# GpSimd waits for VectorE's ramps, and VectorE no longer asks whether GpSimd is idle: a change in the planner of a two-layer attention and gMLP kernel

## The chip, the core and the metric

The kernel runs on one core of a Trainium2 chip. The metric is the device time of one execution in microseconds (us). Five engines are named as the profile names them: PE (TensorE, with PEld for its weight loads), DVE (VectorE), ACT (ScalarE), POOL (GpSimd) and SP (SyncE, which issues the DMAs here). Each engine takes its instructions strictly in the order in which they stand in its stream; an instruction may wait for semaphores that other engines raise.

## What is computed

Two layers, each of multi-query attention (32 heads of 16, one shared key and value head) and a gMLP block, on a sequence of 2048 rows of 512:

```python
def _A_ref(x, wq, wk, wv, wo):
    q = (x @ wq).reshape(B, S, H, Dh).transpose(0, 2, 1, 3)
    k = x @ wk
    v = x @ wv
    scores = jnp.einsum('bhqd,bkd->bhqk', q, k) * Dh ** (-0.5)
    p = _softmax(scores, axis=-1)
    o = jnp.einsum('bhqk,bkd->bhqd', p, v)
    return o.transpose(0, 2, 1, 3).reshape(B, S, H * Dh) @ wo

def _B_ref(x, w_in, w_sp, b_sp, w_out):
    z = _gelu(jnp.einsum('bsd,df->bsf', x, w_in))
    z1 = z[..., :Fh].copy()
    z2 = _layernorm(z[..., Fh:], axis=-1)
    g = jnp.einsum('ts,bsf->btf', w_sp, z2) + b_sp[None, :, None]
    return jnp.einsum('bsf,fd->bsd', z1 * g, w_out)

x = x + _A_ref(_layernorm(x), A_wq, A_wk, A_wv, A_wo)
x = x + _B_ref(_layernorm(x), B_w_in, B_w_sp, B_b_sp, B_w_out)
...
```

The last two lines run twice. With 32 heads, 2048 queries and 2048 keys a layer has 2048 blocks of 128 keys by 512 scores: 4096 in all, each of which needs its exponential.

## The kernel before

**Two ways to an exponential.** TensorE makes a block of scores in a PSUM bank (line 1252, `issue_pack`). Most blocks go to ScalarE, which reads one bank or two neighbouring ones and writes exponentials into slots of the buffer `Pb` (line 1460, `do_exp`). The others go to VectorE and GpSimd. VectorE first reads the bank, adds a constant and writes int16 whose bits are those of a bf16 close to the exponential (line 1374, `first_fn`, called "A" below; it sets the PSUM bank free). Two shifted copies of that slot are then made from SBUF to SBUF (line 1379, `ramp_fn`): these are the **ramps**, tag "S" in the planner. Either VectorE or GpSimd can make a ramp, one slot at a time (128x512) or, where two sources and two free slots lie side by side, two at a time (128x1024, a **pair**; `commit_ramp`, `ramp_pair`). Three weighted copies stand for one exponential, so a block on this way costs TensorE three products with the values and not one (line 1515, `do_pv`).

**The planner.** Nothing is ordered by hand. At build time the class `Sched` plays the whole kernel through with a cost for each operation, and the class `Kernel` decides at each moment what an idle engine takes next (`run` calls `step_act`, `step_dve`, `step_pool`, `step_pe` and `step_sp`). What it commits becomes the stream of that engine; the waits are derived from each task's dependencies (`deps`, and `extra` for reused buffers). In the plan each engine has a time from which it is free (`s.free`). On the chip only the order and the waits are left of it.

**The shared port.** The planner takes VectorE's ramps, its LayerNorm outputs `xn` and `z2n` (the tuple `PORT`) to need something that GpSimd's work needs too. When VectorE commits such a task, GpSimd is planned as occupied until its end (lines after `port =` in `commit`), and VectorE takes a ramp only at a moment when GpSimd is idle in the plan (`s.free["pool"] <= s.t`, line 1711 and its twin further down in `step_dve`). Two thresholds on GpSimd's planned backlog go with that: over `POOL_TOP` VectorE takes a pair ahead of all other work; over `POOL_MAX` it takes any ramp, but only if it has nothing else to do. In the streams, however, no wait keeps GpSimd from starting while VectorE makes its ramps.

**What surrounds it.** GpSimd's stream also holds the reciprocal roots (lines 605 and 606), `xn` (line 628), `z2n` (line 1016) and the last gate products (line 1150). SyncE transposes `xn` by DMA (line 529) for the MLP (lines 988 and 1034), whose gelu runs on ScalarE. The spatial product of the gMLP (line 1095) is added up by VectorE (line 1103). The next layer's attention begins while the last pass of the MLP runs. Where TensorE would be too idle the planner puts in products with a zero operand (line 1634, `keep_warm`). `ACT_LOW` says at which planned backlog of ScalarE TensorE may issue fewer than four blocks of scores at once, `PV_FREE` how many slots of `Pb` must be free before a new accumulation bank is opened, and `SHARE` which part of the blocks goes the VectorE way while TensorE has much else to do.

Of the kernel before, what the change touches and what calls it, by code (L numbers as in the profile page):

```python
# [65 lines left out]
class Task:  # L66
# [3 lines left out]
    def __init__(self, eng, cost, fn, deps=(), prio=5, gate=None, hook=None, mode="full", alts=None, tag=""):  # L70
        self.eng = eng
        self.cost = cost
        self.fn = fn
        self.deps = [d for d in deps if d is not None]
        self.succ = []
        self.prio = prio
        self.ready = 0.0
        self.start = None
        self.done = None
        self.key = None  # L80
        self.val = 0
        self.gate = gate
        self.hook = hook
        self.mode = mode
        self.extra = []
        self.alts = alts
        self.sem = None
        self.armed = False
        self.tag = tag
        self.ramp = None  # L90


class Sched:
# [3 lines left out]
    def __init__(self, nc):  # L97
        self.nc = nc
        self.prog = {e: [] for e in ENGS}
        self.free = {e: 0.0 for e in ENGS}  # L100
        self.cnt = {e: 0 for e in ENGS}
        self.know = {e: {} for e in ENGS}
        self.snap = {}
        self.arm = {e: [] for e in ENGS}
        self.events = []
        self.seq = 0
        self.pe_mode = None
        self.dma_last = [None] * self.NDMA
        self.dma_n = [0] * self.NDMA
        self.t = 0.0  # L110
        self.left = 0
        self.log = []
        self.pe_log = []
        self.after = []
        self.busy = {e: 0.0 for e in ENGS}

    def event(self, t):
# [45 lines left out]
    def commit(self, task, eng=None):  # L163
        t = self.t
        eng = eng or task.eng
        task.eng = eng
        if task.alts is not None:
            task.cost, task.fn = task.alts[eng]
        task.start = t
        if task.hook is not None:  # L170
            task.hook(task)
        cost = task.cost() if callable(task.cost) else task.cost
        occ, lat = cost
        if eng == "pe" and task.mode != self.pe_mode:
            occ += 110
            self.pe_mode = task.mode
        port = eng == "dve" and task.tag in PORT
        if port:
            occ += max(0.0, self.free["pool"] - t)
        end = t + occ  # L180
        self.free[eng] = end
        if port:
            self.free["pool"] = max(self.free["pool"], end)
        self.busy[eng] += occ
        task.done = end + lat
        waits = self._waits(eng, task)
        if eng == "sp":
            k = min(range(self.NDMA), key=lambda i: (self.dma_last[i].done if self.dma_last[i] else -1.0))
            prev = self.dma_last[k]
            if prev is not None:  # L190
                waits += self._wait_on(eng, prev)
            self.dma_n[k] += 16
            task.key, task.val = ("dma", k), self.dma_n[k]
            self.dma_last[k] = task
        else:
            self.cnt[eng] += 1
            task.key, task.val = eng, self.cnt[eng]
        s = dict(self.know[eng])
        if s.get(task.key, 0) < task.val:
            s[task.key] = task.val  # L200
        self.snap[(task.key, task.val)] = s
        self.prog[eng].append((waits, task.fn, task.key, task))
        self.log.append((eng, t, end, task.tag))
        if eng == "pe":
            self.pe_log.append((t, end))
        self.left -= 1
        for s_ in task.succ:
            s_.nopen -= 1
            if s_.nopen == 0:
                self._arm(s_)  # L210
        self.event(end)
        self.event(task.done)
        while self.after:
            self.after.pop(0)()
        return task
# [164 lines left out]
class Kernel:  # L380
# [1 line left out]
    SCORE_CAP = 6  # L382
    WSP_FROM = 25000
    NPS = 32
    PV_FREE = 8
    KT_ACT = 16
    CREDIT = 2
    A_TWO = 0
    KEEP = 8
    PAIRS = 0  # L390
    POOL_TOP = 4000
    HOLD = 200
    A_ADJ = 1
    CAP_LINE = 8000
    RAMP_SHARE = 0.32
# [4 lines left out]
    GP_PRIO = 0.95  # L400
    SP_PRIO = 3.5
    NROT = (2, 2)
    SHARE = 0.32
    SHARE_HI = 0.34
    PE_LINE = 5000
    WARM = 0.6
# [4 lines left out]
    ACT_LOW_R = 0  # L411
    PV_R = 0
    RAMP_SHARE1 = 0.0
    ACT_LOW = 1400
    POOL_MAX = 1400
    DVE_MAX = 1500
    DVE_HIGH = 1800
# [757 lines left out]
    def pack_ready(self):  # L1175
# [4 lines left out]
        room = min(4, len(av), self.score_cap() - self.score_held)  # L1180
        low = self.ACT_LOW if A.full or A.layer == 0 else self.ACT_LOW_R
        if room < (self.FILL_MIN if A.full or A.layer == 0 else self.FILL_R) or room < 4 and self.act_backlog() > low:
# [30 lines left out]
    def issue_pack(self, A, blks, deps, bs):  # L1213
        s = self.s
        k = len(blks)

        x = (self.RAMP_SHARE, self.RAMP_SHARE1)[A.layer] if not A.full else self.SHARE if self.pe_line() > self.PE_LINE else self.SHARE_HI
        self.credit = min(self.credit + k * x, self.CREDIT) if x else 0.0
# [12 lines left out]
        for act in itertools.combinations(sorted(bs, key=lambda b: b.i), len(aj)):  # L1231
            runs = sum(1 for x, y in zip(act, act[1:]) if y.i != x.i + 1)
            rest = sorted([b.i for b in bs if b not in act][:nd] + pend)
            key = (runs - self.A_ADJ * sum(1 for x, y in zip(rest, rest[1:]) if y == x + 1), sum(b.i for b in act))
            if best is None or key < best[0]:
# [242 lines left out]
    def pv_candidate(self):  # L1478
# [5 lines left out]
        for u in self.pv_order:  # L1484
# [4 lines left out]
            if r:  # L1489
                if u.bank is None and (not self.banks.avail() or held >= self.attns[min(self.ai, 1)].nrot_now() and freep >= self.PV_FREE):  # L1490
                    continue
# [101 lines left out]
    def pack_due(self):  # L1593
# [19 lines left out]
        e4 = known[3] if len(known) > 3 else t + 1e5  # L1613
        dry = max(t, s.free["act"]) + 450.0 * len(self.act_q) - self.ACT_LOW
        w = min(e4, max(e2, dry))
# [92 lines left out]
    def step_dve(self):  # L1708
        s = self.s
        k = None  # L1710
        if s.free["pool"] <= s.t + self.PORT_WAIT and self.backlog("pool") > self.POOL_TOP:

            k = self.ramp_pair("dve")
        if k is None:
            k = s.pick("dve", lambda k: k.alts is None or "pool" not in k.alts)

        if k is None and s.free["pool"] <= s.t + self.PORT_WAIT and self.backlog("pool") > self.POOL_MAX:
            k = s.pick("dve")
        if k is None:
            return False  # L1720
        if k.ramp is not None:
            self.commit_ramp(k, "dve")
        else:
            s.commit(k, "dve")
        return True
# [15 lines left out]
    def step_pool(self):  # L1741
        s = self.s
        k = None
        if s.t < s.free["dve"] <= s.t + self.HOLD and self.backlog("pool") > self.POOL_TOP:
            return False
# [138 lines left out]
```

## Time and profile before

| | |
|---|---|
| median of three runs | 1646.38 us (1645.14 to 1647.46) |
| the profiled execution | 1641.84 us, of which the span is 1640.1 us |
| granted TensorE clock | 0.987 |
| busy: PE, DVE, ACT, POOL | 1480.0, 1452.0, 1441.8, 1139.3 us |
| blocks on ScalarE | 923 instructions of two, 956 of one |
| blocks on VectorE's way | 1294, hence 2588 ramps |
| ramps on VectorE | 371 pairs, 111 single |
| ramps on GpSimd | 576 pairs, 583 single |
| zero products (line 1634) | 204 |

"Busy" is the time in which at least one instruction of an engine is recorded as running. VectorE's records overlap: the next one starts some 0.08 us before the one ahead ends, so a row's mean duration is longer than what the instruction adds to the stream. A releaser behind an arrow is what ended an engine's idle time.

### The profile page before, as it was taken

The page shows a single profiled execution, that of the slowest core. Times are in us where ns is not written, and L with a number is a line of the kernel's source. Part 1 is how long each engine was busy: PE and PEld are TensorE (multiplying, and loading weights), DVE is VectorE, ACT ScalarE, POOL GpSimd, SP SyncE. Part 2 cuts the span into 40 slices and gives each one's busy share as a digit, 9 for nine tenths or more (in the row PEclk, how much of TensorE's full clock was granted, in tenths as well). Part 3 has the DMA queues.
Part 4 walks back from the last instruction along what each step waited for, and adds up shares of the span by engine and source line. Part 5 has one row for each costly group of instructions (what it writes and reads, how often), then busy time and mean ns, then how long its engine had stood idle before and what let it go on. Part 6 is the DMA issues. An engine that isn't in the chain of part 4 may idle for free.

```text
span 1640.1 us, 36572 instructions
## 1 busy us (share of the span) xinstructions
PE 1480.0 (90%) x13974; PEld 498.6 (30%) x14104; DVE 1452.0 (89%) x2624; ACT 1441.8 (88%) x2052; POOL 1139.3 (69%) x1410
## 2 busy tenths in 40 slices
PE   6999799999999899989988988999889998999998
PEld 3233232222322223223543322322223222322334
DVE  7899979999799897987874999899997999899977
ACT  5999989999899898987479999899998999899950
POOL 5777768777587677875113767687786877677747
PEclk9999999999999899999999999999999999999999
DMA  9000000100010010101120000020100011101111
GB/s 215 10 8 5 5 10 17 31 20 18 11 27 14 14 27 14 27 14 30 30 44 10 5 5 8 8 46 18 14 15 14 17 24 21 20 14 27 17 33 62
DMA packets 123994, 39.74 MB, mean 24 GB/s; under 512 B 116272, under 2 KB 123312, under 8 KB 123824
## 3 DMA queue, kind: packets, MB, share of 16 engines
q1 hardware_dynamic: 123824, 37.41, 11.3%
q8 instruction: 115, 1.88, 0.5%
q14 instruction: 55, 0.45, 0.1%
HBM read 6.98 MB, written 2.10 MB: 6 GB/s over the span
## 4 chain that ended last, share of the span: by engine, by line
PE 38%; DVE 31%; ACT 22%; issue 4%; POOL 3%; DMA 1%; POOLq 0%; SPq 0%; DVEq 0%; ACTq 0%
ACT Pb L1460 21%; DVE Pb L1374 16%; PE ps_all L1252 11%; PE ps_all L1515 11%; DVE Pb L1379 8%; PE ps_all L1095 6%; PE ps_all L988 3%; PE ps_all L1034 3%; DVE gp L1103 2%; POOL z L1150 2%; PE ps_all L1160 1%; DVE ln_st L614 1%; PE ps_all L773 1%; DVE oT L830 1%; DMA z<-xn 1%
## 5 line engine op out<-in xcount | busy, mean ns | idle before, releaser
L1460 ACT ACTIVATE Pb<-ps_all 128x512 bf16<-128x512 f32 (+1 forms) x1879 | 1345.6, 856 | 78.9 <-PE ps_all L1252 61.8
L1379 POOL TENSOR_SCALAR Pb<-Pb 128x512 int16<-128x512 int16 (+1 forms) x1159 | 987.3, 852 | 340.0 <-DVE Pb L1374 178.1
L1374 DVE TENSOR_SCALAR Pb<-ps_all 128x512 int16<-128x512 f32 x1294 | 842.6, 680 | 86.7 <-PE ps_all L1252 78.5
L1252 PE MATMUL ps_all<-Q,kT 32*128 32x512 bf16 x4096 | 583.6, 388 | 92.8 <-ACT Pb L1460 35.5
L1515 PE MATMUL ps_all<-Pb,V 128*32 128x512 bf16 x6684 | 526.6, 390 | 15.4 <-DVE Pb L1379 4.4
L1252 PEld LDWEIGHTS ps_all<-Q,kT 32*128 32x128 bf16 x4096 | 153.2, 91 | 620.0 <-ACT Pb L1460 361.4
L1379 DVE TENSOR_SCALAR Pb<-Pb 128x1024 int16<-128x1024 int16 (+1 forms) x482 | 260.1, 562 | 9.2 <-PE ps_all L1515 7.9
L1095 PE MATMUL ps_all<-wstr,z 128*128 128x512 bf16 x748 | 194.9, 380 | 19.1 <-issue 5.9
L1515 PEld LDWEIGHTS ps_all<-Pb,V 128*32 128x32 bf16 x6684 | 119.0, 95 | 235.2 <-issue 114.2
L1103 DVE TENSOR_TENSOR gp<-ps_all,gp 128x512 f16<-128x512 f32 x168 | 112.6, 684 | 15.5 <-PE ps_all L1095 14.8
L1095 PEld LDWEIGHTS ps_all<-wstr,z 128*128 128x128 bf16 x840 | 67.1, 97 | 106.6 <-DVE Pb L1374 16.4
L605 POOL TENSOR_SCALAR ln_rs<-ln_mv 128x1 f32<-128x1 f32 (+2 forms) x48 | 10.8, 230 | 86.3 <-DVE ln_mv L615 85.5
L830 DVE CAST oT<-ps_all 128x512 bf16<-128x512 f32 x64 | 43.4, 680 | 19.4 <-PE ps_all L1515 19.4
L1160 PE MATMUL ps_all<-w_out,z 128*128 128x512 bf16 x212 | 55.2, 380 | 3.4 <-POOL z L1150 0.9
L988 PE MATMUL ps_all<-w_in,xnT 128*128 128x448 bf16 x256 | 53.2, 363 | 1.9 <-DVE Pb L1374 1.1
L1048 ACT ACTIVATE z<-ps_all 128x512 bf16<-128x512 f32 (+1 forms) x60 | 31.3, 566 | 22.3 <-PE ps_all L1034 22.3
L1034 PE MATMUL ps_all<-xnT,w_in 128*128 128x512 bf16 (+2 forms) x274 | 50.2, 336 | 0.3
L1001 DVE BATCH_NORM_STATS2 st<-z 128x6 f32<-128x448 bf16 x64 | 36.8, 604 | 11.7 <-ACT z L993 11.5
L614 DVE BATCH_NORM_STATS2 ln_st<-X 128x6 f32<-128x512 bf16 x64 | 43.1, 680 | 3.7 <-DMA X<-in_A_x_dram 3.5
L1103 DVE TENSOR_TENSOR gp<-ps_all,bspc 128x512 f16<-128x512 f32 x56 | 38.3, 686 | 7.0 <-PE ps_all L1095 6.5
L605 POOL TENSOR_SCALAR rs<-mv 128x4 f32<-128x4 f32 (+2 forms) x10 | 2.3, 232 | 58.5 <-DVE mv L1003 58.5
L773 PE MATMUL ps_all<-z,wq 128*128 128x128 bf16 x512 | 40.9, 224 | 1.6 <-DVE Pb L1374 1.3
(69 smaller groups left out, 711.1 us busy)
## 6 DMA issues: line engine op xcount, KB each, us to landing
out_dram<-X SPq DMA_DIRECT2D x16, 128.0 KB, 1.7
w_in<-in_B_w_in_dram SPq DMA_DIRECT2D x1, 1792.0 KB, 13.0
X<-in_A_x_dram SPq DMA_DIRECT2D x3, 512.0 KB, 7.5
bspc<-in_B_b_sp_dram SPq DMA_DIRECT2D x8, 128.0 KB, 3.3
w_out<-in_B_w_out_dram SPq DMA_DIRECT2D x1, 896.0 KB, 12.5
wstr<-in_B_w_sp_dram SPq DMA_TRANSPOSE x40, 4.0
X<-in_A_x_dram SPq DMA_DIRECT2D x2, 256.0 KB, 3.2
wq<-in_A_wq_dram SPq DMA_DIRECT2D x1, 512.0 KB, 4.5
```

The costliest lines, as they stand in the source:

```text
L614: a = self.dve(c_ps(512), lambda e, t=t: e.bn_stats(st[:, t, :], X[:, t, :]), [dep], prio, tag="lnst")
L830: ev = Task("dve", c_ps(512), lambda e, u=u, k=k: e.tensor_copy(self.oT[:, k, :], self.ps32[:, u.bank.i, :]), [self.oT_use[k]], 0.2, tag=" ...
L988: ins = e.matmul(self.ps32[:, b, 0:448], self.xnT2[:, buf, kd, o:o + P], self.w_in[:, kd, FH + h * 448:FH + (h + 1) * 448], start=(kd == 0 ...
L1034: ins = e.matmul(self.ps32[:, b, i * nq:(i + 1) * nq], self.w_in[:, kd, f * P:(f + 1) * P], self.xnT2[:, buf, kd, 0:nq], start=(kd == 0), ...
L1095: ins = e.matmul(self.ps32[:, b, :], self.z2[:, (s0 + i) % 8, f * P:(f + 1) * P], self.wstr[:, sl[i // 4][1] + i % 4, :], start=(i == 0), ...
L1103: return Task("dve", c_ps(512), lambda e: e.tensor_tensor(self.gp[:, tc, f, :], self.ps32[:, bank(), :], src, ALU.add), dps, 1.05, tag="gp")
L1160: ins = e.matmul(self.ps32[:, b, :], self.z1[:, tc, f, o:o + P], self.w_out[:, f, :], start=(f == 0), stop=(f == NF - 1))
L1252: ins = e.matmul(self.ps32[:, jb[i].i, :], self.kT[32 * j:32 * j + 32, u.half, kt * P:(kt + 1) * P], q, tile_position=(32 * j, 0), start=T ...
L1374: return lambda e: e.tensor_scalar(self.Pi[:, dst():dst() + k, :], self.ps32[:, bank:bank + k, :], EBIAS + lo, lo, op0=ALU.add, op1=ALU.max)
L1379: return lambda e: e.tensor_scalar(self.Pi[:, dst():dst() + k, :], self.Pi[:, src():src() + k, :], lo, 1.0, op0=ALU.add, op1=ALU.mult)
L1460: return e.activation(self.Pb[:, s0:s0 + n, :], self.ps32[:, b0:b0 + n, :], ACTF.Exp, scale=ESCALE)
L1515: ins = e.matmul(self.ps32[32 * j:32 * j + 32, u.bank.i, :], self.V[:, var, kt, :], self.Pb[:, sl.i, :], tile_position=(0, 32 * j), start= ...
```

## The change

Only the planner and its constants are edited; no instruction gets a new form.

1. `commit`: when VectorE commits a port task, GpSimd is planned as occupied until that task's result is ready (`end + lat` in place of `end`), and the task is remembered as `port_task`. The next task that GpSimd commits gets it as a dependency, which becomes a semaphore wait in GpSimd's stream. If VectorE commits several ramps before GpSimd's next task, only the last is waited for, which covers the ones ahead of it.
2. `step_dve` asks for `s.pool_end` in place of `s.free["pool"]`, so that the hold that VectorE itself put on GpSimd doesn't end its turn. `pool_end` is set to the end of GpSimd's task when one is committed. The last of the added lines, which is not under an `if`, sets it to 0.0 again at the end of that step of every commit, for any engine. Whenever `step_dve` runs, `pool_end` is therefore 0.0, and both conditions on it hold always. In the same way nothing is ever added to a ramp's planned cost for GpSimd's remaining work.
3. Constants: `POOL_TOP` from 4000 to 3000, with a new `POOL_ON` of 3000 that is used while a `port_task` is open; `PV_FREE` from 8 to 6; `SHARE` from 0.32 to 0.33; `ACT_LOW` from 1400 to 1200.

```diff
         if port:
-            occ += max(0.0, self.free["pool"] - t)
+            occ += max(0.0, self.pool_end - t)
         end = t + occ
         self.free[eng] = end
         if port:
-            self.free["pool"] = max(self.free["pool"], end)
+            self.free["pool"] = max(self.free["pool"], end + lat)
+            self.port_task = task
+        if eng == "pool":
+            self.pool_end = end
+        if eng == "pool" and self.port_task is not None:
+
+            task.extra.append(self.port_task)
+            self.port_task = None
+        self.pool_end = 0.0
...
-    PV_FREE = 8
+    PV_FREE = 6
...
-    POOL_TOP = 4000
+    POOL_TOP = 3000
     HOLD = 200
+    POOL_ON = 3000
...
-    SHARE = 0.32
+    SHARE = 0.33
...
-    ACT_LOW = 1400
+    ACT_LOW = 1200
...
     def step_dve(self):
         s = self.s
         k = None
-        if s.free["pool"] <= s.t + self.PORT_WAIT and self.backlog("pool") > self.POOL_TOP:
+
+        if s.pool_end <= s.t + self.PORT_WAIT and self.backlog("pool") > (self.POOL_TOP if s.port_task is None else self.POOL_ON):
 
             k = self.ramp_pair("dve")
         if k is None:
             k = s.pick("dve", lambda k: k.alts is None or "pool" not in k.alts)
 
-        if k is None and s.free["pool"] <= s.t + self.PORT_WAIT and self.backlog("pool") > self.POOL_MAX:
+        if k is None and s.pool_end <= s.t + self.PORT_WAIT and self.backlog("pool") > self.POOL_MAX:
             k = s.pick("dve")
```

What it makes of the streams can be counted in the two built programs, without a time:

| | before | after |
|---|---|---|
| VectorE: pairs, single ramps | 371, 111 | 204, 645 |
| VectorE: unbroken runs of ramps (of one, of two, longer) | 344 (230, 100, 14) | 571 (308, 249, 14) |
| VectorE: A | 1294 | 1304 |
| GpSimd: pairs, single ramps | 576, 583 | 234, 1087 |
| GpSimd: instructions that wait for VectorE | 867 | 1220 |
| ScalarE: exponentials of two blocks, of one | 923, 956 | 885, 1022 |
| TensorE: products with the values | 6684 | 6704 |
| TensorE: products with zero | 204 | 132 |

More of the change, by code (lines that the diff above doesn't have):

```diff
@@ L182, in commit @@
         if port:
-            self.free["pool"] = max(self.free["pool"], end)
+            self.free["pool"] = max(self.free["pool"], end + lat)
[4 more added lines that the diff above has]
+            task.extra.append(self.port_task)
+            self.port_task = None
+        self.pool_end = 0.0
         self.busy[eng] += occ
```

## The prediction

> **What bounds the kernel now.** I read the page's busy line and its groups first, then the chain that ended last, then the long attention stretches by windows, then VectorE's ramps by shape and one by one.
>
> ```profile
> span 1640.1 us, 36572 instructions
> PE 1480.0 (90%) x13974; PEld 498.6 (30%) x14104; DVE 1452.0 (89%) x2624; ACT 1441.8 (88%) x2052; POOL 1139.3 (69%) x1410
> PE 38%; DVE 31%; ACT 22%; issue 4%; POOL 3%; DMA 1%; POOLq 0%; SPq 0%; DVEq 0%; ACTq 0%
> L1460 ACT ACTIVATE Pb<-ps_all 128x512 bf16<-128x512 f32 (+1 forms) x1879 | 1345.6, 856 | 78.9 <-PE ps_all L1252 61.8
> L1379 POOL TENSOR_SCALAR Pb<-Pb 128x512 int16<-128x512 int16 (+1 forms) x1159 | 987.3, 852 | 340.0 <-DVE Pb L1374 178.1
> L1374 DVE TENSOR_SCALAR Pb<-ps_all 128x512 int16<-128x512 f32 x1294 | 842.6, 680 | 86.7 <-PE ps_all L1252 78.5
> L1379 DVE TENSOR_SCALAR Pb<-Pb 128x1024 int16<-128x1024 int16 (+1 forms) x482 | 260.1, 562 | 9.2 <-PE ps_all L1515 7.9
> ```
>
> Three engines are within 2% of each other in busy time, and the chain passes from one to the next; GpSimd has only 3% of it. Its ramp row shows 340 us of idle time, most of it waiting for VectorE's A. So GpSimd has room; PE, VectorE and ScalarE have little. The attention stretches, 1334 us of the span, show how little:
>
> ```profile
> 41.00:775.00 734.00, 673.15 (x6332) 210.96 (x6383) 661.46 (x1171) 687.95 (x1001) 544.76 (x651) 0.98 0.08 16
> 900.00:1500.00 600.00, 542.64 (x5176) 168.10 (x5222) 550.82 (x958) 566.41 (x806) 449.41 (x531) 0.99 0.09 17
> ```
>
> The columns after the length are PE, PEld, DVE, ACT, POOL busy. ScalarE is busy 1254.4 of 1334 us (94.0%, 80 idle), VectorE 1212.3 (90.9%, 122 idle), POOL 994.2 (74.5%). ScalarE sets the pace there, with VectorE 42 us behind it. Next, what a VectorE ramp costs (timeline, VectorE at 300, 604 and 289 us; GpSimd at 289):
>
> ```profile
> 300.29 0.28 DVE L1379 TENSOR_SCALAR Pb<-Pb 128x512 int16<-128x512 int16 x1
> 300.49 0.68 DVE L1374 TENSOR_SCALAR Pb<-ps_all 128x512 int16<-128x512 f32 x1
> ...
> 603.97 0.75 DVE L1379 TENSOR_SCALAR Pb<-Pb 128x1024 int16<-128x1024 int16 x2
> 604.63 2.50 DVE L1374 TENSOR_SCALAR Pb<-ps_all 128x512 int16<-128x512 f32 x4
> ...
> 288.88 1.60 DVE L1379 TENSOR_SCALAR Pb<-Pb 128x1024 int16<-128x1024 int16 x2
> 290.39 0.67 DVE L1374 TENSOR_SCALAR Pb<-ps_all 128x512 int16<-128x512 f32 x1
> ...
> 289.04 1.15 POOL L1379 TENSOR_SCALAR Pb<-Pb 128x1024 int16<-128x1024 int16 x1 [0.29 <-DVE Pb L1374]
> ```
>
> From start to the next start a single ramp takes 0.20 us, two pairs 0.66 us (0.33 each). But at 288.88 the same two pairs take 1.51 us, and a GpSimd pair that started in between ends at 290.19, just ahead of them: the second pair stood behind it. Reading every VectorE ramp of the trace, an undisturbed record lasts 0.28 us (single) or 0.417 us (pair), and what records exceed that by adds up to 85 us:
>
> ```profile
> L1379 DVE TENSOR_SCALAR Pb<-Pb 128x1024 int16<-128x1024 int16 x371 | 222.1, 618 | 5.9 <-PE ps_all L1515 4.6
> L1379 DVE TENSOR_SCALAR Pb<-Pb 128x512 int16<-128x512 int16 x111 | 40.9, 375 | 3.3 <-PE ps_all L1515 3.3
> ```
>
> (371 x (0.618 - 0.417) + 111 x (0.375 - 0.28) = 85.) Of the 85, 41 us fall on the first ramp of a run (344 heads, 119 ns each) and 42 us on the second (114, 372 ns each). A head that finds GpSimd idle is held 1 ns on average (197), one that finds it running 279 ns (147).
>
> **The change, part by part.**
>
> *The wait on GpSimd* removes what happened at 289 us: GpSimd's next task can't slip between two ramps of a run. That is worth the 42 us of second ramps, if the counted 263 runs of two or more keep together. On GpSimd itself a wait costs the ramp's own time, which it would have spent blocked or in front of the ramp; it starts 0.083 us after VectorE's end (the usual distance in the trace where GpSimd waited), against 0.080 us between two of its own instructions, so nothing more. What queues behind the waiting instruction is the rest of GpSimd's stream: ramps, and the roots and normalized rows of lines 605, 628 and 1016, for which SP's transposes and then the MLP's products wait. The cover is GpSimd's 340 us of idle time, and its own ramp work shrinks: (234 - 576) x 1.069 + (1087 - 583) x 0.637 = -45 us. If the cover failed, a GpSimd chain share of 3% would grow; its 353 added waits at 0.08 us would be 28 us.
>
> *More, smaller ramps on VectorE.* The idle test is gone, so VectorE takes ramps whenever the backlog allows. Undisturbed: 204 x 0.33 + 645 x 0.20 = 196.3 us, against 371 x 0.33 + 111 x 0.20 = 144.6: **+51.7**. Two singles cost 0.40 where a pair costs 0.33; and 200 more of the 2600 ramps are VectorE's.
>
> *Heads held by GpSimd.* 571 runs in place of 344, and nothing asks any more whether GpSimd is idle. Lower bound: 119 ns per head as now, 68 us. Upper: 279 ns, the row of heads that find it running, 159 us. I take 150 ns, a fifth of the way: before, heads one, two or three instructions after the last ramp were held 64, 185 and 50 ns, and 404 of the 571 are such heads now; they are short distances in which GpSimd, which started at the last ramp's end, can have just finished a single ramp. That gives 86 us, **+1** against all 85 of before: the gain on second ramps is spent on heads.
>
> *Ten more blocks for VectorE* (`SHARE`): 10 x 0.651 (842.6 / 1294) = **+6.5** on VectorE; ScalarE loses ten blocks but splits 38 pairs, (885 - 923) x 1.069 + (1022 - 956) x 0.652 = **+2.4**; PE gets 20 products at 79 ns (526.6 / 6684), +1.6, and loses 72 zero products, which filled idle time and count nothing.
>
> *`ACT_LOW`, `PV_FREE`, `POOL_TOP`* have no row. `ACT_LOW` moves when small packs of scores go out: ScalarE waits 61.8 us for scores now; a tenth more or less would be 6 us either way. I take nothing for the three, and keep 6 us for the range.
>
> *What reaches the end.* VectorE gets 51.7 + 1 + 6.5 = +59 us. Of its ramps 8.1% of the span (133 of 260 us, 0.51) lie on the chain that ended last, of its A 15.5% (254 of 843, 0.30), of the exponentials 21.0% (0.26), of the products with values 10.6% (0.33). So 52.7 x 0.51 + 6.5 x 0.30 + 2.4 x 0.26 + 1.6 x 0.33 = **+30 us**. The profiled execution, 1640.1 of span and 1.7 around it, goes to 1671.8; it lay 4.5 under the median, so **1676 us** by the median. With heads at 68 us the sum is +21 (1667), with 159 us +67 (1713).
>
> One rule speaks against moving ramps from GpSimd to VectorE: the Trainium skill, "Perfetto Trace Analysis", section Optimizing Scalar/DVE Operations, says that shifting work between these two may not help, since they share a port that a two-port VectorE operation holds alone. By that rule alone only the port's total counts. With GpSimd's 0.08 us between instructions it goes from 1053 + 145 to 1020 + 196 us, +18, so 1664; the rows differ from it because VectorE itself is nearly full.
>
> **The rivals.**
>
> *The wait pays (faster).* Heads stay as short as the one- and three-distance rows (57 ns x 571 = 33 us), so blocking falls by 52 and pays for the 51.7 of new ramps; VectorE stays at 1452 + 6, and 42 us of late stalls are gone, half of them (0.51) on the chain: 1646 - 21 = 1625. For it: the 42 us are real, and GpSimd's shorter instructions hold the port for less. Against it: ScalarE sets the pace and gets no less work.
>
> *No change.* VectorE's +59 us, some 55 of them in the attention stretches, bring it to 1267 of 1334 us, 95.0%, and a VectorE-bound window shows more is possible (98.5 of 100 us from 900 to 1000). If ScalarE hides it: 1646 + 2 = 1648. Against it: ScalarE's waits come through banks that A frees, and A stands behind the ramps.
>
> *Heads found running (slower still).* If nearly every head meets a running GpSimd instruction, 279 ns x 571 = 159 us; from some 230 ns on, VectorE needs over 97% of the attention stretches at the old length and becomes the bound: 1713, more where pairs (1.04 us) are what it meets.
>
> *The edit does less than it says.* Since `pool_end` is always 0, "while it holds it" isn't tested, and `POOL_ON` equals `POOL_TOP`: the waits alone are new as described. The counts already hold this.
>
> **How the numbers follow.** Forecast 0.47, its own range 1652 to 1712; faster rival 0.30; no change 0.11; heads found running 0.12. A measurement of this kernel can tell about 0.2% (3.3 us) from no change. Slower is the forecast and the last rival, 0.59; within 0.2% most of the no-change case, 0.09; faster 0.30 and a little of that case, 0.32. The range runs from 1621, a little under the faster rival's sum, to 1712, where half of the last rival lies beyond.
>
> **What would show it.** Right: VectorE's busy time near 1510 us, single ramps near 0.28 to 0.40 us a record, second ramps undisturbed, heads held by some 150 ns; GpSimd near 1095 us busy with more waiting for line 1379 on VectorE; ScalarE's idle time ahead of line 1460 grown from 78.9 to about 105 us. Wrong on the fast side: VectorE's ramp group under 245 us in all and ScalarE's idle time shrunk. Wrong on the slow side: records of single ramps at 0.5 us and more, VectorE over 97% in the attention stretches. If second ramps are still blocked, the wait doesn't do what it says.

## The result, and the profile after

The changed kernel takes 1642.25 us (1639.51 to 1645.64, four runs), against 1646.92 for the kernel before, measured beside it. The ratio is **0.9974**, with a 95% interval of 0.9953 to 0.9995: hardly a change, and on the fast side. The forecast was 1676 us, slower.

The page of the changed kernel, the lines that answer to those shown of before (the code's lines have moved by 11 there, so 1390 is `ramp_fn`, 1385 A, 1471 the exponentials):

```profile
span 1640.9 us, 37461 instructions
PE 1497.6 (91%) x14052; PEld 498.9 (30%) x14052; DVE 1502.4 (92%) x3001; ACT 1440.9 (88%) x2080; POOL 1071.7 (65%) x1572
DVE 10%; PE 5%; ACT 3%; POOL 2%; issue 1%; POOLq 0%; DVEq 0%; ACTq 0%
L1471 ACT ACTIVATE Pb<-ps_all 128x512 bf16<-128x512 f32 (+1 forms) x1907 | 1344.0, 833 | 72.9 <-PE ps_all L1263 59.0
L1390 POOL TENSOR_SCALAR Pb<-Pb 128x512 int16<-128x512 int16 (+1 forms) x1321 | 920.7, 697 | 382.8 <-DVE Pb L1390 200.2
L1385 DVE TENSOR_SCALAR Pb<-ps_all 128x512 int16<-128x512 f32 x1304 | 843.2, 676 | 59.0 <-PE ps_all L1263 57.2
L1390 DVE TENSOR_SCALAR Pb<-Pb 128x512 int16<-128x512 int16 (+1 forms) x849 | 340.5, 427 | 4.7 <-PE ps_all L1526 2.0
```

VectorE is busy 50 us more than before (the prediction had 59), and still the span is the same. The largest part of GpSimd's idle time ahead of its ramps is now ended by VectorE's ramps and no longer by A: the new waits at work. The chain line adds up to only 21% of the span; the view lost the chain there, and its shares can't be set against those of before.

The attention stretches by windows (length, then PE, PEld, DVE, ACT, POOL busy):

```profile
41.00:775.00 734.00, 678.63 (x6400) 210.50 (x6398) 686.52 (x1363) 684.73 (x984) 508.74 (x731) 0.98 0.09 17
900.00:1500.00 600.00, 546.90 (x5198) 167.05 (x5195) 570.50 (x1122) 568.10 (x816) 421.48 (x600) 1.00 0.09 17
```

VectorE went from 1212 to 1257 of 1334 us, ScalarE stayed at 1253. The additional VectorE time went into VectorE's idle time, 122 us before and 77 now. ScalarE's idle time ahead of its exponentials, which the prediction expected to grow from 78.9 to about 105 us, fell to 72.9.

VectorE's ramps by shape:

```profile
L1390 DVE TENSOR_SCALAR Pb<-Pb 128x512 int16<-128x512 int16 x645 | 235.7, 389 | 4.4 <-PE ps_all L1526 1.8
L1390 DVE TENSOR_SCALAR Pb<-Pb 128x1024 int16<-128x1024 int16 x204 | 109.0, 547 | 0.3 <-PE ps_all L1526 0.2
```

By the undisturbed 0.28 and 0.417 us a record this is 645 x 0.109 + 204 x 0.130 = 97 us of blocking, in place of 85. Read one by one, its kind has changed entirely: second ramps of a run lose 2 us in all (42 before), heads 95 us (41 before), 166 ns each. A stretch of the changed kernel's timeline shows both, VectorE first, then GpSimd:

```profile
301.60 0.28 DVE L1390 TENSOR_SCALAR Pb<-Pb 128x512 int16<-128x512 int16 x1
301.80 0.68 DVE L1385 TENSOR_SCALAR Pb<-ps_all 128x512 int16<-128x512 f32 x1
302.40 0.89 DVE L1390 TENSOR_SCALAR Pb<-Pb 128x1024 int16<-128x1024 int16 x1
...
301.96 1.05 POOL L1390 TENSOR_SCALAR Pb<-Pb 128x1024 int16<-128x1024 int16 x1 [0.57 <-DVE Pb L1390]
303.37 3.14 POOL L1390 TENSOR_SCALAR Pb<-Pb 128x512 int16<-128x512 int16 x4 [0.36 <-DVE Pb L1390]
```

GpSimd waits until VectorE's single ramp has ended at 301.88 and starts at 301.96. VectorE makes one A and comes to its next ramp at 302.40, in the middle of GpSimd's pair, since the plan no longer asks whether GpSimd is idle; the record lasts 0.89 us in place of 0.417. GpSimd's next one waits for it in turn.

### The profile page after: what moved, and what is told of

The parts are those of the page before. It is cut to its first block, busy times and chain, and to the rows that moved or that the text cites. A ratio compares the mean times of both kernels' runs of the same rounds, so it can differ in the third digit from the quotient of the medians.

```text
span 1640.9 us, 37461 instructions
## 1 busy us (share of the span) xinstructions
PE 1497.6 (91%) x14052; PEld 498.9 (30%) x14052; DVE 1502.4 (92%) x3001; ACT 1440.9 (88%) x2080; POOL 1071.7 (65%) x1572
## 5 line engine op out<-in xcount | busy, mean ns | idle before, releaser
L1471 ACT ACTIVATE Pb<-ps_all 128x512 bf16<-128x512 f32 (+1 forms) x1907 | 1344.0, 833 | 72.9 <-PE ps_all L1263 59.0
L1390 POOL TENSOR_SCALAR Pb<-Pb 128x512 int16<-128x512 int16 (+1 forms) x1321 | 920.7, 697 | 382.8 <-DVE Pb L1390 200.2
L1263 PE MATMUL ps_all<-Q,kT 32*128 32x512 bf16 x4096 | 576.0, 387 | 84.5 <-DVE Pb L1385 34.8
L1390 DVE TENSOR_SCALAR Pb<-Pb 128x512 int16<-128x512 int16 (+1 forms) x849 | 340.5, 427 | 4.7 <-PE ps_all L1526 2.0
L1106 PE MATMUL ps_all<-wstr,z 128*128 128x512 bf16 x840 | 214.1, 381 | 8.1 <-DVE Pb L1385 2.5
L1171 PE MATMUL ps_all<-w_out,z 128*128 128x512 bf16 x224 | 59.3, 380 | 2.3 <-POOL z L1161 0.9
L1004 ACT ACTIVATE z<-ps_all 128x448 bf16<-128x448 f32 x64 | 31.2, 539 | 18.1 <-PE ps_all L999 18.1
```

Source lines behind the costliest of these rows:

```text
L1106: ins = e.matmul(self.ps32[:, b, :], self.z2[:, (s0 + i) % 8, f * P:(f + 1) * P], self.wstr[:, sl[i // 4][1] + i % 4, :], start=(i == 0), ...
L1171: ins = e.matmul(self.ps32[:, b, :], self.z1[:, tc, f, o:o + P], self.w_out[:, f, :], start=(f == 0), stop=(f == NF - 1))
L1263: ins = e.matmul(self.ps32[:, jb[i].i, :], self.kT[32 * j:32 * j + 32, u.half, kt * P:(kt + 1) * P], q, tile_position=(32 * j, 0), start=T ...
L1390: return lambda e: e.tensor_scalar(self.Pi[:, dst():dst() + k, :], self.Pi[:, src():src() + k, :], lo, 1.0, op0=ALU.add, op1=ALU.mult)
L1471: return e.activation(self.Pb[:, s0:s0 + n, :], self.ps32[:, b0:b0 + n, :], ACTF.Exp, scale=ESCALE)
```

## The experiments

The question was which parts cancelled. A wait leaves the order of the streams alone, so it can be put in or taken out by itself; the idle test and the constants change the order. Each kernel was compared with the kernel before on the same chip, which gave 1643 to 1645 us there.

**The wait alone** (e1_wait_only), on the kernel before (`port_task` also starts as `None`, not shown):

```diff
         if port:
             self.free["pool"] = max(self.free["pool"], end)
+            self.port_task = task
+        if eng == "pool" and self.port_task is not None:
+            task.extra.append(self.port_task)
+            self.port_task = None
```

> The kernel before, its streams in the same order, with GpSimd's wait alone: 344 of its instructions now wait for the last ramp of a run (388 waits are raised). If VectorE's time hides in its idle time (theory 'slack'): second ramps lose nearly all of their 42 us of blocking, VectorE's busy time falls by about 40 us to 1412, and the time moves by less than 0.3% (1642 to 1651). If VectorE's time reaches the end by its share of the chain (theory 'chain share', that of the prediction): 42 x 0.51 = 21 us less, 1626.

It took 1603.83 us, ratio **0.9762** (0.9744 to 0.9779): 39 us less, more than either theory had. A small part of that goes with the granted clock, which was 0.986 to 0.989 in its runs and 0.976 to 0.986 in those of the kernel before on that chip: where both had 0.986, it was 1605.93 us against 1640.05 and 1640.08, 34 us less. Its page and the attention stretches (here 1384 is `ramp_fn`, 1465 the exponentials):

```profile
PE 1498.8 (94%) x14104; PEld 499.7 (31%) x14104; DVE 1391.2 (87%) x2624; ACT 1430.8 (89%) x2052; POOL 1112.7 (69%) x1410
ACT 47%; PE 39%; DVE 7%; POOL 3%; issue 3%; DMA 1%; SPq 0%; POOLq 0%; DVEq 0%; ACTq 0%
L1465 ACT ACTIVATE Pb<-ps_all 128x512 bf16<-128x512 f32 (+1 forms) x1879 | 1334.7, 900 | 52.3 <-PE ps_all L1257 46.6
L1384 DVE TENSOR_SCALAR Pb<-Pb 128x1024 int16<-128x1024 int16 (+1 forms) x482 | 187.4, 411 | 10.4 <-PE ps_all L1520 8.3
```

The same 482 ramps have a mean record of 411 ns, where it was 562. Blocking fell from 85 to 12.5 us, and not at the second ramps alone (42 to 1): heads, too, went from 119 to 33 ns each, 41 to 11 us in all. VectorE's share of the chain went from 31% to 7%, ScalarE's from 22% to 47%. The attention stretches, in the same windows (PE, PEld, DVE, ACT, POOL busy after the length):

```profile
41.00:775.00 734.00, 698.91 (x6565) 223.40 (x6565) 653.67 (x1208) 687.62 (x1011) 533.82 (x656) 0.99 0.09 18
900.00:1500.00 600.00, 566.82 (x5312) 171.03 (x5313) 535.84 (x984) 576.58 (x822) 450.83 (x546) 0.99 0.10 18
```

VectorE is busy 1190 of 1334 us here, ScalarE 1264, TensorE 1266: now these two set the pace. In the timeline of this kernel, VectorE then GpSimd, a run of two passes undisturbed and GpSimd's next one starts 0.09 us after it:

```profile
284.73 0.75 DVE L1384 TENSOR_SCALAR Pb<-Pb 128x1024 int16<-128x1024 int16 x2
...
285.57 2.44 POOL L1384 TENSOR_SCALAR Pb<-Pb 128x1024 int16<-128x1024 int16 x3 [0.93 <-DVE Pb L1384]
```

**The changed kernel without the wait** (e2_no_wait):

```diff
         if eng == "pool" and self.port_task is not None:
-            task.extra.append(self.port_task)
             self.port_task = None
```

> The changed kernel, its streams in the same order, without GpSimd's wait (564 waits lowered): GpSimd can start between two ramps of a run again. There are 278 ramps that follow another one; at the 372 ns each that second ramps had before, at most 103 us of blocking come back, less since GpSimd's instructions are shorter now (some 60 us). Slack: VectorE goes to about 1560 us busy, 96 to 98% of the attention stretches, and the time rises by 0 to 1% (1642 to 1659). Chain share: 60 x 0.51 = 31 us more, 1673, and the wait is what paid for the ramps.

1655.48 us, ratio 1.0087 (1.0062 to 1.0113), so the wait is worth some 1.1% in the changed order as well. VectorE's ramps:

```profile
L1389 DVE TENSOR_SCALAR Pb<-Pb 128x512 int16<-128x512 int16 x645 | 243.4, 401 | 3.3 <-PE ps_all L1525 0.4 <-PE ps_all L1262 0.3
L1389 DVE TENSOR_SCALAR Pb<-Pb 128x1024 int16<-128x1024 int16 x204 | 123.4, 617 | 0.0
```

645 x 0.121 + 204 x 0.200 = 119 us of blocking, 22 more than with the wait; I had expected 60. 31 us of it are second ramps again; the heads stay at 87, and run e5 below shows that the emptied test causes most of that. The time lies in the range of the theory 'slack' and not near the 1673 of 'chain share', but this settles little: 22 us of blocking came back and not 60, and each cost more than either theory had, 19 us of time for 22.

**The wait after every second run only** (e12_half_wait), on the kernel before:

```diff
         if eng == "pool" and self.port_task is not None:
-            task.extra.append(self.port_task)
+            self.port_n = getattr(self, "port_n", 0) + 1
+            if self.port_n % 2:
+                task.extra.append(self.port_task)
             self.port_task = None
```

> The kernel before, its streams in the same order, with GpSimd's wait after every second run of VectorE's ramps only (185 of its instructions wait for a ramp in place of 344). If each wait is worth what it saves in blocking (73 us of blocking and 39 us of time for all of them): blocking near 45 to 55 us and the time near 1625 (1618 to 1632). If the plan's order is restored only when all runs are guarded, GpSimd gets ahead at the unguarded ones and the gain is under a quarter: 1635 or more.

1614.37 us, ratio 0.9831 (0.9801 to 0.9862). VectorE's ramps:

```profile
L1386 DVE TENSOR_SCALAR Pb<-Pb 128x1024 int16<-128x1024 int16 (+1 forms) x482 | 213.9, 466 | 9.9 <-PE ps_all L1522 8.3
```

Undisturbed, these 371 pairs and 111 singles would be 185.8 us of records; 482 x 0.466 = 224.6 is 39 us of blocking. So 46 us less blocking went with 28 us less time, 0.6 to one; with all waits it was 73 for 39, 0.54 to one. Half the waits give some 70% of the gain for 63% of the blocking: on this order the gain follows the blocking. The expected ranges were a little too high.

**The wait and the open test, with the old constants** (e3_gate_off_old_consts), the changed kernel with the following (`PV_FREE` stays at 6)

```diff
-    POOL_TOP = 3000
+    POOL_TOP = 4000
...
-    POOL_ON = 3000
-    SHARE = 0.33
-    ACT_LOW = 1200
+    POOL_ON = 4000
+    SHARE = 0.32
+    ACT_LOW = 1400
```

> The changed kernel with the constants of before (ACT_LOW 1400, SHARE 0.32, POOL_TOP and POOL_ON 4000; only PV_FREE stays at 6): GpSimd waits, the idle test stays away; 714 single ramps and 160 pairs on VectorE in 591 runs, 1292 A. The wait alone gave 1604. If the missing idle test costs the rest (theory 'gate'): 90 to 105 us of blocking at the heads of runs as in the changed kernel, 1635 to 1655. If the constants cost it (theory 'constants'): 1600 to 1615.

1649.89 us, ratio 1.0036 (1.0014 to 1.0058). VectorE's ramps:

```profile
L1390 DVE TENSOR_SCALAR Pb<-Pb 128x512 int16<-128x512 int16 x714 | 265.1, 395 | 8.6 <-PE ps_all L1526 5.4 <-DVE Pb L1385 0.5
L1390 DVE TENSOR_SCALAR Pb<-Pb 128x1024 int16<-128x1024 int16 x160 | 83.3, 531 | 0.9 <-PE ps_all L1526 0.9
```

714 x 0.115 + 160 x 0.114 = 100 us of blocking; 98 of it are at heads. Without the idle test all that the wait gave is lost again, with these constants too.

**The wait, the idle test and the new constants** (e4_wait_new_consts): the diff of e1 and

```diff
-    PV_FREE = 8
-    POOL_TOP = 4000
-    SHARE = 0.32
-    ACT_LOW = 1400
+    PV_FREE = 6
+    POOL_TOP = 3000
+    SHARE = 0.33
+    ACT_LOW = 1200
```

> The kernel of before with GpSimd's wait and the idle test, and with the four new constants (403 pairs and 105 single ramps on VectorE, 1305 A, 352 runs). Gate: blocking stays under 25 us and the time at 1595 to 1615, as with the wait alone. Constants: 1635 or more.

1609.0 us, ratio 0.9776 (0.9753 to 0.9800), 13 us of blocking. Where the wait and the idle test are in place, the constants do nothing that can be told here.

**A test that works** (e5_no_reset), the changed kernel without the line that empties `pool_end`:

```diff
             task.extra.append(self.port_task)
             self.port_task = None
-        self.pool_end = 0.0
```

> The changed kernel without the one line that sets pool_end to 0.0 at every commit, so that VectorE's test for GpSimd's planned end works and several pairs in a row are possible (446 pairs, 71 single, 320 runs, 40 of them of three or more). Gate: heads find GpSimd idle again, blocking under 30 us, VectorE some 1390 us busy, 1590 to 1612, at most as long as the wait alone (1604). Constants: 1635 or more, since these are the changed kernel's.

1611.22 us, ratio **0.9787** (0.9760 to 0.9813). Against the changed kernel's 0.9974, this one line is 1.9% of the time, 31 us. The time is in the expected range but not, as expected, at most that of the wait alone; the two intervals overlap. VectorE is busy 1404.6 us (1390 expected). VectorE's ramps here, whose blocking is 7 us when read one by one:

```profile
L1389 DVE TENSOR_SCALAR Pb<-Pb 128x1024 int16<-128x1024 int16 (+1 forms) x517 | 197.6, 412 | 8.8 <-PE ps_all L1525 6.1
```

**The same with all constants of before** (e11_no_reset_old_consts): that diff, the constants set back as in e3, and `PV_FREE` to 8.

> The changed kernel without the line that sets pool_end to 0.0 and with all constants of before (POOL_ON 4000): GpSimd waits, VectorE's test for GpSimd's planned end works (441 pairs, 61 single, 318 runs). With these constants the wait alone gave 1604, with the new ones the working test gave 1611. If the constants are worth the same everywhere: 1600 to 1606. If the turn of several pairs has a price or a gain of its own, it shows as a distance from 1604 of over 5 us.

1614.24 us, ratio 0.9831 (0.9802 to 0.9861), 7 us of blocking. So runs of three and more, which both of these have and the wait alone hardly has, bring no gain of their own: with blocking as low as it gets, neither is faster than the wait alone. This one even lies ten us above it, which by the expectation would be a price of the turn of several pairs. But e5, with the same turn, lies only some 4 us above it by the ratios, so the cause stays open; e11 has 1039 single exponentials, where the wait alone has 956.

**More VectorE work without more blocking** (e10_split_pairs), on e1: each of VectorE's pairs is given out as two singles.

```diff
-                f = Task(eng, (c_pool if eng == "pool" else c_4x)(1024), self.ramp_fn(v, lambda: i, lambda: o, 2), k.deps + p.deps, tag="S")
+                rf = self.ramp_fn(v, lambda: i, lambda: o, 2)
+                if eng == "dve":
+                    ra, rb = self.ramp_fn(v, lambda: i, lambda: o, 1), self.ramp_fn(v, lambda: i + 1, lambda: o + 1, 1)
+
+                    def rf(e):
+                        ra(e)
+                        return rb(e)
+                f = Task(eng, (c_pool if eng == "pool" else c_4x)(1024), rf, k.deps + p.deps, tag="S")
```

> The kernel with GpSimd's wait alone (1604), with each of VectorE's 371 pairs given out as two single ramps in the same place: 371 x (0.40 - 0.33) = 26 us more undisturbed VectorE work that holds the port, and no new runs. If such work reaches the end like blocking does, with half of it: 1617. If VectorE's idle time takes it: 1604 to 1608.

1608.5 us, ratio 0.9775 (0.9752 to 0.9797), against 0.9762 for e1: about 2 us more, and by the two intervals some 5 us either way. The ramps:

```profile
L1384 DVE TENSOR_SCALAR Pb<-Pb 128x512 int16<-128x512 int16 x853 | 216.7, 303 | 9.4 <-PE ps_all L1527 7.6
```

VectorE is busy 20 us more (1410.9) where 26 were expected, 7 us of it blocking (853 x 0.023 = 20, in place of 12.5). By the prediction's share of 0.51 the expected 26 us would have cost 13; about 2, at most some 7, reached the end. The chain of this run:

```profile
ACT 37%; PE 34%; DVE 20%; POOL 4%; issue 4%; DMA 2%; SPq 0%; POOLq 0%; ACTq 0%
```

VectorE has 20% of it, where e1 has 7%. Its ramps alone went from 14 to 59 chain microseconds, nearly all of them of ramps that nothing blocked, for about 2 us of time. So a share of the chain need not be a price.

**Small extra instructions ahead of A** (e6_pad_half, e7_pad_all), on the kernel before, ahead of every second A or of every one (`% 1`); they fill a column of a tile of their own:

```diff
+        self.pad = self.sb([P, 16], FP32, "pad")
+        self.pad_n = 0
...
-        return lambda e: e.tensor_scalar(self.Pi[:, dst():dst() + k, :], self.ps32[:, bank:bank + k, :], EBIAS + lo, lo, op0=ALU.add,
-                                         op1=ALU.max)
+        def fn(e):
+            self.pad_n += 1
+            if self.pad_n % 2 == 0:
+                e.memset(self.pad[:, self.pad_n % 16:self.pad_n % 16 + 1], 0.0)
+            return e.tensor_scalar(self.Pi[:, dst():dst() + k, :], self.ps32[:, bank:bank + k, :], EBIAS + lo, lo, op0=ALU.add,
+                                   op1=ALU.max)
+        return fn
```

> The kernel before with one tiny extra VectorE instruction (a fill of one column of a tile of its own) ahead of every second A, 647 in all, which the planner knows nothing of; at some 60 ns each 39 us more on VectorE. Slack: the time rises by less than 0.5% (under 1655). Chain share: A's 0.30 to ramps' 0.51 of 39 us, 12 to 20 us more (1658 to 1667).

> The same ahead of every A, 1294 in all, some 78 us more on VectorE, which would fill two thirds of its 122 idle us in the attention stretches. Slack: more than twice what half of it costs, since the idle time runs out: 1650 to 1680. Chain share: 23 to 40 us more (1670 to 1687), twice what half of it costs.

1653.63 us (ratio 1.0061, 1.0046 to 1.0076) and 1655.77 us (1.0080, 1.0063 to 1.0098). A line of the second:

```profile
L1379 DVE MEMSET pad<- 128x1 f32 x1294 | 76.3, 59 | 0.0
```

and A's line in it:

```profile
L1380 DVE TENSOR_SCALAR Pb<-ps_all 128x512 int16<-128x512 f32 x1294 | 850.3, 684 | 85.1 <-issue 72.2 <-POOL z L1018 5.2 <-POOL Pb L1386 0.7
```

This is a weak experiment. The fills wait for nothing, so part of them ran while VectorE waited for scores anyway: with all of them VectorE's busy time grew by 15 us only, and A had 72 us of idle time ahead of it that no releaser explains. Busy and unexplained idle time together grew by 50 and 87 us, for 11 and 13 us of time. Neither theory had the second dose cost so little more than the first, but both times lie in the ranges of 'slack' and below those of 'chain share': 11 us for 38 us of fills and 13 for 76, 0.3 and 0.2 to one. Blocking hardly changed (86 and 90 us).

Side by side, blocking read from each profile one ramp at a time:

| kernel | wait | idle test | blocking, us | ratio |
|---|---|---|---|---|
| before | no | yes | 85 | 1 |
| half the waits (e12) | half | yes | 39 | 0.9831 |
| split pairs (e10) | yes | yes | 19 | 0.9775 |
| new constants (e4) | yes | yes | 13 | 0.9776 |
| **wait alone (e1)** | yes | yes | 12.5 | **0.9762** |
| `pool_end` kept (e5) | yes | on `pool_end` | 7 | 0.9787 |
| `pool_end` kept, old constants (e11) | yes | on `pool_end` | 7 | 0.9831 |
| changed kernel | yes | none | 97 | 0.9974 |
| changed, old constants (e3) | yes | none | 100 | 1.0036 |
| changed, no wait (e2) | no | none | 119 | 1.0087 |

Every kernel with 39 us of blocking or less is faster than every kernel with 85 or more by over 1%. Within the two groups the order of the times is not that of the blocking: the changed kernel has 12 us more of it than the kernel before and is no slower, and 7 us are not better than 12.5.

## Why the prediction was wrong

**Right: what the change does to VectorE.** Busy time 1502 us (forecast 1511), undisturbed records as costed, second ramps freed (2 us left of 42), heads held 166 ns (150, a choice between two bounds of which the lower was none, see below), the net of blocking +11 us (+1). GpSimd had room, though the wait was miscounted: not 353 waits were added, but on the same order some 550 of GpSimd's instructions now wait for a later VectorE instruction than they would, nearly all of which waited for VectorE anyway.

**Wrong: "What reaches the end".** This step multiplied all of it, 51.7 us of undisturbed ramps and the blocking, by 0.51, the ramps' share of the chain. But the 133 chain microseconds are not of one kind. Laid against the ramps one by one, the chain of before passes through 108 of the 162 ramps that were held by over 0.1 us, and 95 of the 133 us are theirs; 61 of the 85 us of blocking lie on it. Most of what the chain held of ramps was there in blocked ramps. The chain of the kernel before, around the example that the prediction showed (start, length, what):

```profile
288.48 0.34 PE ps_all L1252 x2
288.82 0.06 issue
288.88 1.61 DVE Pb L1379 x2
290.48 0.04 issue
290.53 0.61 PE ps_all L1515 x8
```

After the scores the chain runs through the two pairs, with GpSimd's in between, and the products with the values that follow on it start only at 290.53. With the blocking gone, VectorE's share falls to 7% (e1); where unblocked ramps take it up to 20% again (e10), 20 us more VectorE time cost about 2. The term that I put at 26 us (51.7 x 0.51) would be some 5 to 14 by what additional VectorE work cost in e10, e7 and e6 (0.1 to 0.3 to one), an estimate; without it the sum is +4. From the kernel before to e3 undisturbed ramps grow by 51 us, blocking by 15 and the time by 6 (2 to 10): at e1's 0.54 the blocking alone would be 8, which leaves the 51 nothing to explain. The rows for it were there: ScalarE paced the stretches, with VectorE's 122 idle us beside it. The no-change rival said so and got 0.11; that its 1648 came close is in part luck, for it had neither the gain nor the loss that follow. The port's total, which the prediction put at +18 us of time, was no guide either: 200 more ramps on VectorE, and the time fell by 4.

**Wrong: what the wait is worth.** It was credited with the second ramps alone, 42 x 0.51 = 21 us. It gave 39. "Lower bound: 119 ns per head as now" was no lower bound: those heads, too, were held by a GpSimd that had run ahead of the plan, and the wait alone brings them to 33 ns.

**Wrong: where the loss is.** It is not that VectorE gets more ramps. The idle test and the wait belong together: the plan places a run where GpSimd is idle, and the wait keeps GpSimd from running past that place. With the test emptied, the plan itself puts runs into the middle of GpSimd's instructions, and the wait can't help against one that has started. The prediction set this loss against the blocking of before and came to +1; set against the 7 us of e5, where the same kernel keeps `pool_end`, it is 90 us of blocking and 31 us of time.

So at some 1645 us, one part at a time: the wait -39 (e1), the new constants +2 (e1 to e4), the test on `pool_end` with the longer hold +2 (e4 to e5), the line that empties it +31 (e5 to the changed kernel), together -4; the two in the middle are within the noise. A gain of over 2% and a loss of nearly 2% had cancelled. The prediction had smaller ones, and between them a cost that the runs don't show. The faster rival had the right sign by a sum that did not happen (blocking down by 52), the rival "the edit does less than it says" named the emptied test, and I took its cost for counted.

Three things stay open. The parts don't simply add: by way of e3 they are -39, then +45 (e1 to e3), then -10 for the constants (e3 to the changed kernel). Of the 45, 34 lie between e11 and e3, which differ in the line that empties the test and in `PV_FREE`, and 11 between e1 and e11. And the constants seem to help by 0.6% where the test is empty and not where it works; they were not tried one by one, and part of it may go with the granted clock, which was 0.973 to 0.991 in the runs of e3 and 0.985 to 0.990 in those of the changed kernel: at 0.989 to 0.991 e3 took 1643 to 1644 us and the changed kernel 1640 to 1642. Nor is the price of blocking one number: 0.34 of its length from e5 to the changed kernel, 0.5 to 0.6 on the order of before, 0.85 from the changed kernel to e2.

## What to carry to other kernels

Where two engines exclude each other and a plan keeps them apart, put the exclusion into the streams as a wait, and keep the plan's own test beside it: here the missing wait cost 2.4%, and the emptied test took nearly as much back. Before a row's chain share is used as the price of more work on that row, ask which of its instructions are on the chain: blocked ones have a price of their own (0.3 to 0.9 of the blocking here), and undisturbed work on an engine with idle time may cost much less (0.1 to 0.3 here). When a result is near zero, try each part alone; the best kernel of this study, 1604 us, is the kernel before with the wait alone.

## What the runs showed of the hardware that was not expected

Between two of VectorE's ramps that stand directly behind one another, GpSimd gets its turn: without the wait 67 of the 114 second ramps before were held by over 0.1 us, 372 ns on average over all of them, though the second one's record begins before the first one's ends. With the wait the mean is 6 ns. And the blocking is mutual but unequal: VectorE's records grew by 85 us in all, while GpSimd's ramps lasted 637 and 1069 ns on average before and 620 and 1047 ns with the wait, 583 x 0.017 + 576 x 0.022 = 23 us.
